# Windowed attention and a gated feed-forward on one core: first loads in one queue, four output parts and some deferred work at other places in a hand-written order

## The chip, the cores and the metric

One core of a Trainium2 chip. The metric is the device time of one execution in microseconds (us). Kernel before: median 245.3 us of 4 runs (244.92 to 245.75).

## The reference, cut to what matters

Attention over 4 batches, 8 heads, 768 positions and 64 numbers a head. A position sees the 96 positions up to itself and the first 8 ("global") ones. A linear bias by distance is added to the scores. The result, 3072 tokens of 512 numbers, goes through a feed-forward with 1536 inner numbers:

```python
scores = scale * np.matmul(q, k.transpose(0, 1, 3, 2)) + bias   # bias = -slope[h] * dist
a = softmax(np.where(keep, scores, -1e9))                       # keep: global or local
x = (a @ v).transpose(0, 2, 1, 3).reshape(B * S, H * D)
g = x @ w_gate
out = (g * sigmoid(g) * (x @ w_val)) @ w_out
```

## The kernel before, in words

**Tiles and blocks.** The 3072 tokens are 8 tiles of 384, two for each batch (the code's `b`). A tile's feed-forward has 12 blocks of 128 inner numbers, written (t, f) below. `gate_or_val` (L549) does one block in two calls: the first multiplies the tile by the gate weights (four matmuls of 128x384, tile `gps`), ScalarE takes a tanh of it (`th`, L558), and VectorE makes the SiLU (`sl`, L560); the second multiplies by the value weights (four matmuls, `vps`) and VectorE writes the product to `hT` (L564). `out_part` (L568) multiplies three blocks of a finished tile by `wo`; four parts make 128 tokens of output in the one bank `o0`, ScalarE copies that to `osb` (L582), and SP's queue stores it (L583). A tile has 12 parts.

**Attention beside it.** While one tile goes through the feed-forward, the attention of the next batch is put between its blocks as steps: `tr` transposes q and k of a pair of heads (TensorE, then copies on ScalarE and VectorE); `sc` multiplies keys by queries for two or three units (pair, key range); `va` makes, for four heads, the sums of the weights (`den`) and the two weighted sums of the values (`num`), and VectorE turns them into tokens: `dT` (L449), `dR` (L450), `rb` (L455) and two `xT` (L475). For batch 0, `sch` does bias and scores of a pair's second half, `trh` its transposes. From batch 1's second half on, `vas` does both groups of heads in one step.

**Order.** The order of every engine is the order in which the Python code issues. `stretches` lists the blocks with the number of output parts after each (`ff`, L766), and a dictionary of steps by place: (t, f) is behind block f and its parts, (t, f, n) ahead of the n-th part. Work that a step puts off lies in the list `later`: exponentials of the units behind the first, the multiplication by the masks (VectorE), and the four VectorE pieces of `va`. `run_later(1)` takes one piece: ahead of each gate, each value product and each output part. `take` empties the list ahead of a new step.

```python
            for which in range(2):
                run_later(1)
                gate_or_val(t, f, which, NC if t == 0 and f < 2 else 0)
```

**Banks.** `gps` and `vps` take turns in three PSUM banks x0 to x2 (`spare`); steps take turns in a0 to a3 (`banks`). A three-unit `sc` takes two of the spare banks for its first unit. From (0,9) to (1,2) `widen` (L803) lends the a banks to the feed-forward, so that seven take turns; `narrow` (L811) ends that, and gps(1,2) takes the bank that vps(1,0) used.

**Loads.** POOL's queue issues the converting loads in the order of the code, at most eight under way: weights by quarters of the blocks (`load_w`), `wo` in four loads of three blocks' rows each (`load_wo(g)`, g 0 to 3), q and k of batch 1 (`load_qk`), global rows (`load_globals`) and values (`load_v_rest`). The very first loads are unconverted: k32 on SP's queue, the identity and q32 on ScalarE's. SP's queue also stores the outputs and copies the global rows of v (`copy_globals`).

Of the kernel before, what the change touches and what calls it, by code (L numbers as in the profile page):

```python
# [37 lines left out]
def kernel(  # L38
# [12 lines left out]
    nc = tc.nc  # L51
# [48 lines left out]
    q32 = sb2.tile([128, 2, J2 * D], FP32, name="q32", tag="qst")  # L100
# [4 lines left out]
    def half_of(src, half, h0, h1):  # L105
        return src[0, h0:h1, TB * half:TB * half + TB, :].rearrange(
            "h (p j) d -> p h (j d)", p=128)
# [1 line left out]
    vG32 = sb.tile([NG, H, D], FP32, name="vG32")  # L109
    nc.sync.dma_start(out=k32, in_=half_of(k, 0, 0, 2))  # L110
    nc.scalar.dma_start(out=ident, in_=const_dr.ap()[:, 0:128])
    nc.scalar.dma_start(out=q32, in_=half_of(q, 0, 0, 2))
    nc.sync.dma_start(out=dist[:, 0:2 * WIN], in_=const_dr.ap()[:, 128:128 + 2 * WIN])
    nc.sync.dma_start(out=vG32, in_=v[0, :, 0:NG, :].rearrange("h p d -> p h d"))
    nc.sync.dma_start(out=dist[:, 2 * WIN:], in_=const_dr.ap()[:, 128 + 2 * WIN:])
# [31 lines left out]
    def stage(b):  # L147
        qst[b] = sb2.tile([128, H, J * D], FP16, name="qst", tag="qst")
        kst[b] = sb2.tile([128, H, J * D], FP16, name="kst", tag="kst")

    def load_qk(b, h0, h1):
        for st, src in ((kst[b], k), (qst[b], q)):
            nc.gpsimd.dma_start(
                out=st[:, h0:h1, :],
                in_=src[b, h0:h1].rearrange("h (p j) d -> p h (j d)", p=128))
# [23 lines left out]
    def load_globals():  # L179
        for dst, src in ((kG, k), (vG[:, 1:], v)):  # L180
            nc.gpsimd.dma_start(
                out=dst.rearrange("p b h d -> p (b h) d"),
                in_=src[1:, :, 0:NG, :].rearrange("b h p d -> p (b h) d"))
# [33 lines left out]
    def load_wo(g):  # L217
        nc.gpsimd.dma_start(
            out=wo[:, 3 * g:3 * g + 3, :],
            in_=moe_w_out[384 * g:384 * g + 384].rearrange("(f p) d -> p f d", p=128))  # L220
# [18 lines left out]
    def banks(name, dt=FP32):  # L239
        return [bank(name, dt) for _ in range(2)]  # L240

    def spare(name, dt=FP32):
        tag = state["x"][gv.get("n", 0) % len(state["x"])]
        gv["n"] = gv.get("n", 0) + 1
        return single(name, tag, dt)

    def single(name, tag, dt=FP32):
        return ps.tile([128, 512 if dt == FP32 else 1024], dt, name=name, tag=tag)
# [8 lines left out]
    def run_later(n):  # L257
        for _ in range(n):
            if later:
                later.pop(0)()  # L260
# [277 lines left out]
    def products(t, f, which, c0, c1, dst=None):  # L538
        if f == 0 and which == 0 and c0 == 0:
            hTs[t] = sb2.tile([128, NFF, TB], FP16, name="hT", tag="hT", bufs=3)  # L540
        if c0 == 0:
            if dst is None:
                dst = spare("gv"[which] + "ps")
            gv[f, which] = dst
        w = (wg, wv)[which]
        for c in range(c0, c1):
            nc.tensor.matmul(  # L547
                gv[f, which][:, 0:TB], lhsT=w[:, c, 128 * f:128 * f + 128],
                rhs=x_of(t)[:, c, :],  # L549
                start=(c == 0), stop=(c == NC - 1))  # L550

    def gate_or_val(t, f, which, c0=0):
        products(t, f, which, c0, NC)
        dst = gv.pop((f, which))

        if which == 0:
            th = sb2.tile([128, TB], FP32, name="th", tag="th")
            nc.scalar.activation(out=th, in_=dst[:, 0:TB], func=AF.Tanh, scale=0.5)  # L558
            sl = sb2.tile([128, TB], FP32, name="sl", tag="sl")
            nc.vector.scalar_tensor_tensor(  # L560
                out=sl, in0=th, scalar=1.0, in1=dst[:, 0:TB], op0=AluOp.add, op1=AluOp.mult)
            gv["sl"] = sl
        else:
            nc.vector.tensor_mul(hTs[t][:, f, :], dst[:, 0:TB], gv["sl"])  # L564
# [37 lines left out]
    for c in range(3):  # L602
        load_v_rest(0, c)
    nc.gpsimd.dma_start(
        out=vCut[NG:NG + cut], in_=v[0, :, 3 * KC:TB, :].rearrange("h p d -> p h d"))
# [41 lines left out]
    load_w(8, 12)  # L647
    load_wo(0)
    load_wo(1)
    stage(1)  # L650
    load_qk(1, 0, 4)
    load_globals()
    load_wo(2)
    load_wo(3)
    load_qk(1, 4, 8)
    for c in range(NCH):
# [29 lines left out]
    def sc(b, *units):  # L686
        def step():
            for i, (hp, bk, *other) in enumerate(units):
                pair = pairs[b + 1 if other else b, hp]
                on_vector = pair.b < 2 or bk < 2 or hp % 2 == 0  # L690
                exps, mask = pair.scores(
                    bk, nc.vector if on_vector else nc.gpsimd,
                    [spare("sc") for _ in range(2)] if len(units) == 3 and i == 0
                    else banks("sc"))
                if i == 0:
                    exps()
                else:
                    later.append(exps)
                later.append(mask)
        return step  # L700

    def va(b, g, half):
        return lambda: quads[b, g].values(half, bank, nc.vector)
# [4 lines left out]
    def tr(b, hp):  # L708
        return pairs[b, hp].transposes

    def trh(h0, h1, by_engine):
        def step():
            b0, b1 = single("trs", "o0", FP16), spare("trs", FP16)
            (a, b), (c, d) = [(t[:, 0:TB], t[:, TB:2 * TB]) for t in (b0, b1)]
            k_eng = V if by_engine else A
            pair_of = [(h0, (c, a)), (h1, (d, b))] if by_engine else [(h0, (b, a)), (h1, (d, c))]
            for hp, tr in pair_of:
                pairs[0, hp].turn_half(1, tr)
            for hp, tr in pair_of:
                pairs[0, hp].copy_half(1, tr, k_eng, A)  # L720
        return step

    def sch(hp):
        def step():
            p = pairs[0, hp]
            scs = [p.bias(1, 0), p.bias(1, 1)]
            for which in range(2):
                p.scores_half(1, which, scs[which], which == 1)
        return step
# [9 lines left out]
    def first(t, b):  # L739
        return {(t, 2): [tr(b, 0), tr(b, 1)],  # L740
                (t, 4): [sc(b, (0, 0), (0, 1), (1, 0))],
                (t, 6): [tr(b, 2), tr(b, 3)],
                (t, 7): [sc(b, (1, 1), (2, 0), (2, 1))],
                (t, 9): [sc(b, (3, 0), (3, 1))],
                (t, 10): [va(b, 0, 0)],
                (t, 11, 1): [va(b, 1, 0)]}

    def both(t, b):

        n = b + 1  # L750
        return {(t, 0): [sc(b, (0, 2), (1, 2), (2, 2)), fetch(n, 0, 1)],
                (t, 5): [sc(b, (3, 2), (0, 0, n), (1, 0, n)), fetch(n, 2, 3)],
                (t, 8): [vas(b, 1)],
                (t + 1, 0): [sc(n, (0, 1), (1, 1), (2, 0))],
                (t + 1, 4): [sc(n, (2, 1), (3, 0), (3, 1))],
                (t + 1, 8): [vas(n, 0)]}

    def second(t, b):
        return {(t, 0): [sc(b, (0, 2), (1, 2))], (t, 3): [sc(b, (2, 2), (3, 2))],
                (t, 7): [vas(b, 1)]}  # L760

    half1 = {(0, 1): [trh(0, 1, False)], (0, 2): [sch(0)],
             (0, 3): [sch(1), trh(2, 3, True)], (0, 5): [sch(2)], (0, 6): [sch(3)],
             (0, 7): [va(0, 0, 1)], (0, 8): [va(0, 1, 1)]}

    def ff(t, f0, f1, n_out=(0,)):  # L766
        return [(t, f, n_out[(f - f0) % len(n_out)]) for f in range(f0, f1)]

    stretches = [
        (ff(0, 0, 12), half1),  # L770
        (ff(1, 0, 5, (0, 0, 0, 0, 1)) + ff(1, 5, 11, (1,)) + [(1, 11, 5)], first(1, 1)),
        (ff(2, 0, 12, (1,)) + ff(3, 0, 12, (1,)), both(2, 1)),
        (ff(4, 0, 12, (1,)) + ff(5, 0, 12, (1,)), both(4, 2)),
        (ff(6, 0, 12, (1,)), second(6, 3)),
        (ff(7, 0, 12, (1,)), {})]

    loads, after = {}, {}

# [40 lines left out]
    def take(step_list):  # L819
        run_later(len(later))  # L820
        for step in step_list:
            step()

    for tiles, steps in stretches:
        for t, f, n_out in tiles:
            for ld in loads.pop((t, f), []):
                ld()
            if f == 0:
                while any(fn.__name__ in ("spread", "spread_first", "scale") for fn in later):
                    run_later(1)  # L830
            for which in range(2):
                run_later(1)
                gate_or_val(t, f, which, NC if t == 0 and f < 2 else 0)
                for fn in after.pop((t, f, which), []):
                    fn()
            for n in range(n_out):
                if (t, f, n) in steps:
                    take(steps.pop((t, f, n)))
                run_later(1)
                out_part(*outs.pop(0))  # L840
            if (t, f) in steps:
                take(steps.pop((t, f)))
        assert not steps
# [40 lines left out]
```

The softmax here doesn't subtract the row's maximum and nothing guards it: scores larger than these inputs give would overflow.

## Time and profile before

| | before |
|---|---|
| median of 4 runs | 245.3 us |
| the profiled execution: its own time / its span | 244.92 / 243.1 us |
| PE busy | 234.6 us, 96% of the span |
| VectorE (DVE) busy | 165.7 us, 68% |
| ScalarE (ACT) busy | 129.6 us, 53% |
| POOL busy | 96.6 us, 40% |
| granted TensorE clock | 9 tenths or more in all 40 slices |

The span runs from the first to the last instruction of the profiled execution. In a timeline row stand the start, the length, engine, line and operation, out<-in with shapes, the number of instructions merged into the row, and in brackets the idle time of the engine just ahead of it with what ended it. A row of the waits names who waited for whom, the total, how often, and the longest. A row's length in the timeline runs to the end of its last instruction; on PE, consecutive groups overlap in these lengths, and the distance between the starts of two rows tells what a group takes of the engine.

Where the stages lie: PE's first transposes start at 4.71 us, the first matmul of the feed-forward at 15.16, tile 1 begins at about 41.6, tile 2 at 74.4, and the last 24 matmuls begin at 237.3.

### The profile page before, as it was taken

The page shows a single profiled execution, that of the slowest core. Times are in us where ns is not written, and L with a number is a line of the kernel's source. Part 1 is how long each engine was busy: PE and PEld are TensorE (multiplying, and loading weights), DVE is VectorE, ACT ScalarE, POOL GpSimd, SP SyncE. Part 2 cuts the span into 40 slices and gives each one's busy share as a digit, 9 for nine tenths or more (in the row PEclk, how much of TensorE's full clock was granted, in tenths as well). Part 3 has the DMA queues.
Part 4 walks back from the last instruction along what each step waited for, and adds up shares of the span by engine and source line. Part 5 has one row for each costly group of instructions (what it writes and reads, how often), then busy time and mean ns, then how long its engine had stood idle before and what let it go on. Part 6 is the DMA issues. An engine that isn't in the chain of part 4 may idle for free.

```text
span 243.1 us, 6052 instructions
## 1 busy us (share of the span) xinstructions
PE 234.6 (96%) x2428; PEld 135.4 (56%) x2428; DVE 165.7 (68%) x354; ACT 129.6 (53%) x295; POOL 96.6 (40%) x117
## 2 busy tenths in 40 slices
PE   8899899799999999999999999999999999999994
PEld 4455466455555556555565556555655565555543
DVE  5665649879796768776786658776785568555610
ACT  5637586786864565366346464367336634333221
POOL 8899664737990000996062252700032213000000
PEclk9999999999999999999999999999999999999999
DMA  8999999999999574899319877941101101110122
GB/s 150 164 184 197 180 206 197 205 152 124 135 130 153 120 133 99 55 153 143 56 8 144 143 141 87 77 59 44 46 0 46 43 6 40 44 42 2 44 89 87
DMA packets 84612, 25.10 MB, mean 103 GB/s; under 512 B 72816, under 2 KB 81640, under 8 KB 84584
## 3 DMA queue, kind: packets, MB, share of 16 engines
q0 software_dynamic: 65296, 14.05, 67.0%
q1 hardware_dynamic: 18728, 10.30, 16.7%
q8 instruction: 19, 0.31, 0.5%
q10 hardware_dynamic: 560, 0.36, 0.5%
q14 instruction: 9, 0.07, 0.1%
HBM read 28.67 MB, written 6.29 MB: 144 GB/s over the span
## 4 chain that ended last, share of the span: by engine, by line
PE 84%; DMA 6%; POOL 5%; DVE 2%; issue 1%; ACT 0%; DVEq 0%; POOLq 0%
PE gps L547 25%; PE vps L547 24%; PE ops L576 23%; DMA wv<-in_moe_w_val_dram 4%; PE sc L379 3%; PE num L439 3%; DMA vS<-in_v_dram 3%; PE den L439 2%; POOL q L119 1%; PE trs L273 1%; POOL wg L213 1%; PE ops L592 1%; POOL k L119 1%; POOL wv L213 1%; DVE xT L475 1%
## 5 line engine op out<-in xcount | busy, mean ns | idle before, releaser
L547 PE MATMUL gps<-xT,wg 128*128 128x384 f16 x376 | 77.3, 327 | 2.6 <-DVE hT L564 1.7
L560 DVE SCALAR_TENSOR_TENSOR sl<-th,gps 128x384 f32<-128x384 f32 x94 | 51.9, 553 | 40.3 <-ACT th L558 39.8
L547 PE MATMUL vps<-xT,wv 128*128 128x384 f16 x376 | 76.6, 326 | 0.7 <-DMA wv<-in_moe_w_val_dram 0.6
L558 ACT ACTIVATE th<-gps 128x384 f32<-128x384 f32 x94 | 46.9, 499 | 53.2 <-PE gps L547 51.9
L576 PE MATMUL ops<-wo,hT 128*128 128x512 f16 x276 | 72.8, 379 | 0.0
L564 DVE TENSOR_TENSOR hT<-vps,sl 128x384 f16<-128x384 f32 x94 | 52.1, 554 | 8.8 <-PE ops L576 0.5
L547 PEld LDWEIGHTS <-wg 128*128 128x128 f16 x384 | 35.0, 98 | 33.8 <-issue 3.6
L547 PEld LDWEIGHTS <-wv 128*128 128x128 f16 x384 | 37.5, 98 | 26.8 <-issue 1.3
L576 PEld LDWEIGHTS <-hT 128*128 128x128 f16 x276 | 26.9, 98 | 23.9
L387 ACT ACTIVATE at<-sc 128x432 f16<-128x432 f32 x72 | 33.2, 539 | 11.5 <-PE sc L379 11.5
L516 POOL TENSOR_TENSOR xT<-ns,rb 128x384 f16<-128x384 f32 x10 | 9.8, 994 | 66.0 <-DVE rb L455 55.0
L171 POOL DMA_DIRECT2D vS<-in_v_dram x28 | 24.7, 899 | 5.0 <-DMA kst<-in_k_dram 3.0
L582 ACT ACTIVATE osb<-ops 128x512 f32<-128x512 f32 x23 | 13.7, 597 | 22.0 <-PE ops L576 22.0
L398 POOL TENSOR_TENSOR at<-at,masks 128x864 f16<-128x864 f16 x4 | 7.3, 1819 | 23.8 <-ACT at L387 19.1
L398 DVE TENSOR_TENSOR at<-at,masks 128x864 f16<-128x864 f16 x20 | 12.1, 605 | 5.7 <-ACT at L387 5.7
L194 POOL DMA_DIRECT2D kst<-in_k_dram x16 | 14.0, 896 | 2.9 <-PE gps L547 2.3
L361 ACT ACTIVATE at<-sc 128x432 f16<-128x432 f32 (+2 forms) x32 | 11.7, 447 | 5.0 <-PE sc L350 4.8
L194 POOL DMA_DIRECT2D qst<-in_q_dram x16 | 13.8, 891 | 0.2 <-issue 0.2
L512 ACT COPY ns<-num 128x384 f32<-128x384 f32 x20 | 8.1, 493 | 7.9 <-PE num L439 7.9
L439 PE MATMUL num<-at,vS 128*32 128x216 f16 (+6 forms) x560 | 11.1, 226 | 0.0
L395 DVE TENSOR_TENSOR at<-at,masks 128x432 f16<-128x432 f16 x24 | 8.1, 378 | 4.4 <-ACT at L387 4.4
L449 DVE STREAM_TRANSPOSE dT<-den 128x384 f32<-128x384 f32 x16 | 9.3, 581 | 1.6 <-PE den L439 1.1
(74 smaller groups left out, 178.5 us busy)
## 6 DMA issues: line engine op xcount, KB each, us to landing
out_dram<-osb SPq DMA_DIRECT2D x23, 256.0 KB
vS<-in_v_dram POOLq DMA_DIRECT2D x24, 120.0 KB, 5.3
wo<-in_moe_w_out_dram POOLq DMA_DIRECT2D x4, 384.0 KB, 10.5
qst<-in_q_dram POOLq DMA_DIRECT2D x16, 96.0 KB, 4.3
kst<-in_k_dram POOLq DMA_DIRECT2D x16, 90.0 KB, 4.2
wg<-in_moe_w_gate_dram POOLq DMA_DIRECT2D x4, 256.0 KB, 7.7
wv<-in_moe_w_val_dram POOLq DMA_DIRECT2D x4, 256.0 KB, 8.1
kst<-in_k_dram POOLq DMA_DIRECT2D x2, 384.0 KB, 11.7
```

Of the source, the lines that this page charges most:

```text
L171: nc.gpsimd.dma_start(out=vSs[b][NG:NG + n, c, :, :], in_=v[b, :, KC * c:KC * c + n, :].rearrange("h p d -> p h d"))
L194: nc.gpsimd.dma_start(out=st[b][p0:p0 + n, h // 2, :, h % 2, :], in_=src[b, h, 0:n * J].rearrange("(t p) d -> p t d", p=n))
L361: nc.scalar.activation(out=at[:, hi, 0:col + n], in_=sc[hi][:, 0:col + n], func=AF.Exp, scale=scale)
L387: nc.scalar.activation(out=at[:, hi, :], in_=sc[hi][:, 0:BANK], func=AF.Exp, scale=scale)
L398: mul_eng.tensor_mul(at, at, m[:, :, o:o + BANK])
L439: nc.tensor.matmul(dst[r, o:o + n], lhsT=ones[:, 0:32] if side is None else vals[:, 4 * g + j, side::2], rhs=pairs[b, 2 * g + j // 2].at[c ...
L547: nc.tensor.matmul(gv[f, which][:, 0:TB], lhsT=w[:, c, 128 * f:128 * f + 128], rhs=x_of(t)[:, c, :], start=(c == 0), stop=(c == NC - 1))
L558: nc.scalar.activation(out=th, in_=dst[:, 0:TB], func=AF.Tanh, scale=0.5)
L560: nc.vector.scalar_tensor_tensor(out=sl, in0=th, scalar=1.0, in1=dst[:, 0:TB], op0=AluOp.add, op1=AluOp.mult)
L564: nc.vector.tensor_mul(hTs[t][:, f, :], dst[:, 0:TB], gv["sl"])
L576: nc.tensor.matmul(ops, lhsT=hTs[t][:, f, 128 * i:128 * i + 128], rhs=wo[:, f, :], start=(f == 0), stop=(f == NFF - 1))
L582: nc.scalar.mul(out=osb, in_=ops, mul=0.5)
```

## The change

The edits, each on its own:

1. q32's load is issued on SP's queue, behind k32's, and no longer on ScalarE's.
2. The third load of `wo` is issued ahead of batch 1's first q and k loads and its global rows.
3. Output parts behind (0,10), (0,11), (1,0) and (1,2): four that were elsewhere. Before, tile 1 had one part behind (1,4) to (1,10) each and five behind (1,11). Now it has one behind (1,0), (1,2) and (1,4) to (1,9), two behind (1,10) and (1,11). Tile 7 has none behind (7,10) and (7,11).
4. In tiles 0 and 1 a put-off piece is run behind each gate and each value product, with the operations that follow them, and no longer ahead of them.
5. Batch 1's last three steps of its first half (scores of pair 3, and the values of both groups) stand one block earlier, and the two-unit `sc` of batch 1 takes spare banks for its first unit.

```diff
-    nc.scalar.dma_start(out=q32, in_=half_of(q, 0, 0, 2))
+    nc.sync.dma_start(out=q32, in_=half_of(q, 0, 0, 2))
...
     load_wo(1)
+    load_wo(2)
     stage(1)
     load_qk(1, 0, 4)
     load_globals()
-    load_wo(2)
     load_wo(3)
...
-                    [spare("sc") for _ in range(2)] if len(units) == 3 and i == 0
+                    [spare("sc") for _ in range(2)] if i == 0 and (len(units) == 3 or b == 1)
...
-                (t, 9): [sc(b, (3, 0), (3, 1))],
-                (t, 10): [va(b, 0, 0)],
-                (t, 11, 1): [va(b, 1, 0)]}
+                (t, 8): [sc(b, (3, 0), (3, 1))],
+                (t, 9): [va(b, 0, 0)],
+                (t, 10, 1): [va(b, 1, 0)]}
...
-        (ff(0, 0, 12), half1),
-        (ff(1, 0, 5, (0, 0, 0, 0, 1)) + ff(1, 5, 11, (1,)) + [(1, 11, 5)], first(1, 1)),
+        (ff(0, 0, 10) + ff(0, 10, 12, (1,)), half1),
+        (ff(1, 0, 4, (1, 0)) + ff(1, 4, 10, (1,)) + ff(1, 10, 12, (2,)), first(1, 1)),
...
-        (ff(7, 0, 12, (1,)), {})]
+        (ff(7, 0, 10, (1,)) + ff(7, 10, 12), {})]
...
             for which in range(2):
-                run_later(1)
+                if t > 1:
+                    run_later(1)
                 gate_or_val(t, f, which, NC if t == 0 and f < 2 else 0)
+                if t < 2:
+                    run_later(1)
```

## The prediction

> Notation: (t, f) is feed-forward block f of token tile t; gps and vps are its gate and value products, th, sl and hT the tanh, SiLU and product behind them. Starts are on the clock of the profiled execution of before.
>
> **What bounds it now.** I read the shares of the span first: PE is busy 234.6 of 243.1 us, at full granted clock in every slice. PE's matmuls are the same before and after, so only PE's waits can change the time. Next, the waits of PE:
>
> ```profile
> PE gps L547 <- DVE hT L564: 1.7, 1, 1.7
> PE warm L612 <- DVE kT L131: 1.2, 1, 1.2
> PE gps L547 <- DMA wg<-in_moe_w_gate_dram: 0.7, 2, 0.5
> PE vps L547 <- DMA wv<-in_moe_w_val_dram: 0.6, 1, 0.6
> ```
>
> The timeline of PE places them: weights at 20.0, 26.25 and 27.71; DVE's wait at (1,2):
>
> ```profile
> 43.59 0.81 PE L547 MATMUL vps<-xT,wv 128*128 128x384 f16 x4
> 46.14 0.81 PE L547 MATMUL gps<-xT,wg 128*128 128x384 f16 x4 [1.74 <-DVE hT L564]
> ```
>
> Four such matmuls begin 0.65 after the four before them, though a row shows 0.81: the next could have begun at 44.24, so the wait costs 1.90, not 1.74. (The Trainium skill, "Perfetto Trace Analysis", section "Tensor Engine Instruction", says that a matmul's end is estimated, not observed. By the row's end the wait is 1.74 and my sum 0.16 higher; the spacing of starts decides.)
>
> A second loss is not listed, because it lies inside a group, at (2,0):
>
> ```profile
> 74.38 1.10 PE L547 MATMUL gps<-xT,wg 128*128 128x384 f16 x4
> 75.32 0.81 PE L547 MATMUL vps<-xT,wv 128*128 128x384 f16 x4
> ```
>
> 0.94 from start to start in place of 0.65: 0.29 lost, to the last xT of VectorE (74.08, 1.03 long). Both losses are VectorE running late after it has turned sums into tokens. Its timeline ahead of the first:
>
> ```profile
> 35.84 0.57 DVE L449 STREAM_TRANSPOSE dT<-den 128x384 f32<-128x384 f32 x1
> 36.45 0.23 DVE L450 RECIPROCAL dR<-dT 128x12 f32<-128x12 f32 x1
> 36.68 0.55 DVE L560 SCALAR_TENSOR_TENSOR sl<-th,gps 128x384 f32<-128x384 f32 x1
> ...
> 40.56 1.03 DVE L475 TENSOR_TENSOR xT<-ns,rb 128x384 f16<-128x384 f32 x2
> 41.51 0.55 DVE L560 SCALAR_TENSOR_TENSOR sl<-th,gps 128x384 f32<-128x384 f32 x1
> ...
> 45.53 0.56 DVE L564 TENSOR_TENSOR hT<-vps,sl 128x384 f16<-128x384 f32 x1
> ```
>
> It has no gap from 34.71 to 47.2. 36.68 is sl(0,8), 41.51 sl(0,9), 45.53 hT(1,0), which frees the bank that gps(1,2) takes when the pool narrows back to three. Four blocks take 4.58: 1.12 each.
>
> **Part by part.** The instruction order of the changed kernel gives the moves.
>
> *First loads.* q32's issue (0.55 on ACT) goes behind k32's (0.46 on SP): issued at about 1.26 instead of 1.15; dist and vG32 0.5 later. Bytes are the same, and PE still meets the wv load that ends at 27.7: PE idles 0.47 and 0.65 just ahead of it, which absorbs a later head; an earlier head only waits longer. I take 0, with plus or minus 0.55, the moved issue, as ends. (The Trainium skill, "DMA: Bandwidth & Descriptors", section "Queues, rings and completion order", says that a DMA engine takes turns between queue rows. That speaks against one row: k32 and q32 would get one turn against POOL's, not two. ScalarE's conversion of q32 now starts 3.4 after its issue, VectorE's of k32 2.9; if q32 had to wait for half of k32's time the head would slip, as an estimate from this page and those rows, by some 1, and the sum by 0, as the 1.12 covers it.)
>
> *Put-off work behind tanh, tile 0.* Two effects.
> (a) ACT. sch(3)'s last biases need the banks that sch(2)'s two 432-column exponentials empty. Now four exponentials run in a row:
>
> ```profile
> 30.36 1.52 ACT L361 ACTIVATE at<-sc 128x264 f16<-128x264 f32 x4 [0.97 <-PE sc L350]
> 31.74 0.53 ACT L558 ACTIVATE th<-gps 128x384 f32<-128x384 f32 x1
> ```
>
> After, th(0,6) stands ahead of the last two. It can start when gps(0,6), 30.45 to 31.11, is done plus 0.2: 31.31. The exponentials start 0.39 later at 31.70 and 32.11, and end (0.54 each) at 32.24 and 32.65. The bias matmuls, now due at about 32.09 and 32.27, wait until 32.29 and 32.70: **+0.43** on PE.
> (b) DVE. dT and dR of (0,8), which fill 35.84 to 36.68 now, go behind sl(0,8). That waits for th(0,8), at 36.64 plus 0.43 = 37.07: DVE idles 1.2. From there sl .47, dT .61, dR .23, hT .47, rb .68, two xT .92, dT .61, dR .26, rb .68, two xT .95 (starts to starts in the rows above) = 5.88: sl(0,9) at 42.98, not 41.51. hT(1,0) ends 4.58 later: 47.56.
>
> *Four outputs.* One in each of (0,10), (0,11), (1,0), (1,2). The first three, 0.65 each, stand ahead of gps(1,2): PE arrives at 44.24 + 1.95 + 0.43 = 46.62 and finds the bank at 47.61 (0.05 of semaphore): wait 0.99 instead of 1.90: **-0.91**. The outputs are only moved: two are taken from (1,11), two from tile 7, so their own 2.60 net to nothing. Their cover: hT(0,11) ends at 46.4, needed at 48.9. wo(2), issued in kst's slot, should land near 41.6, when kst does now; needed at 44.7. wo(3) lands at 47.7 as now, needed at 48.9. If that cover of 1.2 is gone, PE waits one for one. The block-1 rows of q land about 2.2 later, at 45.6, for transposes at 49.7. On SP the three vS copies (44.11) now stand behind the first output's store, to about 50; va needs them near 66. In tile 7 two fewer outputs leave (7,11) bare: vps(7,11) needs sl(7,10), 1.97 after its gps, and arrives at 1.95: 0.
>
> *Tile 1's end.* From the transposes of (1,2) on I keep before's clock; everything is 2.13 later and two outputs ahead. hT(1,7), now behind no mask but a later sl, delays gps(1,8) by 0.08. At (1,8) the mask goes between sl and hT: sl 62.74, two masks 63.21 to 63.80, hT to 64.36. The scores of pair 3, one block sooner, take two of the three spare banks, so gps(1,9) needs the bank of hT(1,8): 64.41 against an arrival at 63.89: **+0.52** (with the 0.08, 0.60). The boundary: now
>
> ```profile
> 68.97 0.58 DVE L449 STREAM_TRANSPOSE dT<-den 128x384 f32<-128x384 f32 x1
> 69.58 0.23 DVE L450 RECIPROCAL dR<-dT 128x12 f32<-128x12 f32 x1
> 70.19 0.55 DVE L560 SCALAR_TENSOR_TENSOR sl<-th,gps 128x384 f32<-128x384 f32 x1 [0.38 <-ACT th L558]
> ```
>
> After: DVE runs dry at 67.92, waits for th(1,10) and starts sl(1,10) at 68.74. Then without a gap sl, dT, dR, hT, rb, two xT, dT, dR, sl(1,11), rb, hT(1,11): the last two xT end at 74.92 and 75.42. PE is at gps(2,0) at 73.58 (block 11 and two outputs since va), so vps(2,0) starts at 75.63 instead of 74.23: 1.40 lost, now 0.29: **+1.11**. The block sooner is paid back, because block 11's sl and hT (1.1) now lie in the chain and only two outputs, not four, cover it.
>
> *Later tiles.* Two outputs ahead, the output's copy (0.60 on ACT) falls between the second and third unit's exponentials after sc at (2,0), (3,0), (3,4), (4,0), (5,0), (5,4). Now:
>
> ```profile
> 78.64 1.79 ACT L387 ACTIVATE at<-sc 128x432 f16<-128x432 f32 x4
> 80.28 0.54 ACT L558 ACTIVATE th<-gps 128x384 f32<-128x384 f32 x1
> ```
>
> The copy starts at 79.55, 0.2 after its matmuls, and holds th to 80.87, sl(2,2) ends at 81.98, and vps(2,3) at 81.94 needs that bank: 0.05 to 0.09, six times: **+0.4** (ends 0 and 0.9).
>
> **Sum.** +0.43 - 0.91 + 0.60 + 1.11 + 0.4 = +1.6. The profiled execution took 244.92 (span 243.1 and 1.8 around it): 246.5. It is the fastest of four, whose median is 245.3; from that 246.9. I give 246.6.
>
> **Rivals**, from the median of 245.3.
> *Faster:* the reordering costs VectorE nothing. Place: its two dry spells ahead of sl(0,8) and sl(1,10), price 1.2 and 0.8. It decides once th(0,8) starts near 35.6 instead of 36.6 and th(1,10) as early against its work. Then sl(0,9) is at 41.9, the wait of 1.90 is gone, and the boundary loses 0.6: -1.90 + 0.3, nothing else: 243.7. Against: th follows gps by 0.2 in each row, and gps comes no sooner.
> *Cancelled:* the bank waits at sch(3) and (1,9) and the six small ones don't show (slack under 0.1 in my walk would do for the six, earlier exponentials for the others). (b) shrinks with (a). Left: -0.91 + 1.11 = +0.2: 245.5. For: each is a difference of two walked times. Against: no other bank is free there.
> *Worse, from the forecast's 246.6:* wo(3) or the first loads also slip past their cover, by 1 to 1.5: 247.9. Against: 1.1 to 1.2 of cover.
>
> **Numbers.** Chances: forecast 0.60 (half width 0.7), cancelled 0.20, faster 0.13, worse 0.07. A measurement can tell 0.3%, 0.74 us, from no change, so slower begins at 246.04. Forecast's low tail gives a little to "same": faster 0.13, same 0.23, slower 0.64. The range leaves out the faster case and the worse one's far part: 244.7 to 247.8.
>
> **What to look for after.** PE's wait on hT at (1,2) near 1.0, not 0; the bias matmuls of L339 at about 32 waiting for ACT; gps(1,9) waiting for hT; the group gps(2,0) 2 us long; VectorE idle ahead of sl(0,8) and sl(1,10); wv still landing near 27.7. I am wrong if VectorE has no such gaps, if gps(2,0) starts vps within 0.3 of its due time, or if a wait on wo appears.

## The result, and the profile after

The changed kernel takes 246.05 us (median of 43 runs, 245.50 to 246.78), the kernel before 244.75 us on the same chips (median of 64). The ratio is 1.0048, with a 95% interval of 1.0039 to 1.0057: 1.2 us slower (0.95 to 1.4). The 245.3 us that stood for the kernel before were the median of four runs, 0.55 above that of the 64.

The profiled execution of the changed kernel took 246.01 us, span 244.2, against 244.92 and 243.1: +1.1 in both. The granted clock was 1.000 in both. So its trace can be set beside the earlier one, time by time. Four rows of the waits of PE after (who waited for whom, total, times, longest):

```profile
PE trs L299 <- DMA q<-in_q_dram: 1.1, 1, 1.1
PE num L439 <- DVE dT L449: 0.6, 1, 0.6
PE gps L547 <- DVE hT L564: 0.4, 1, 0.4
PE gps L547 <- DVE xT L475: 0.4, 1, 0.4
```

The listed 1.7 for hT at (1,2) is gone. Three listed waits on VectorE stand in its place, and each is shorter than it. The list alone would promise a faster kernel; it leaves out what lies inside groups. (The q of the first row is the second load of q, on POOL's queue, and not q32.) The timeline of PE, after, in three places. First sch(3) and the values of batch 0:

```profile
31.88 1.28 PE L339 MATMUL sc<-dist,slopeI 128*128 128x72 f16 x6
33.09 0.48 PE L350 MATMUL sc<-qT,kT 64*128 64x72 f16 x10
...
37.34 0.49 PE L439 MATMUL den<-at,ones 128*32 128x72 f16 x20
38.42 0.79 PE L439 MATMUL num<-at,vS 128*32 128x72 f16 x40 [0.59 <-DVE dT L449]
```

The six bias matmuls of L339 take 1.21 from start to start; before, they took 0.69 (31.76 to 32.45): 0.52 lost, without a bracket. The second num matmuls wait for dT, which before they did not:

```profile
36.70 0.49 PE L439 MATMUL den<-at,ones 128*32 128x72 f16 x20
37.02 0.78 PE L439 MATMUL num<-at,vS 128*32 128x72 f16 x40
```

They start 1.08 after den, and before 0.32: 0.76 lost, where the bracket says 0.59.

Around (1,2):

```profile
46.95 0.81 PE L547 MATMUL vps<-xT,wv 128*128 128x384 f16 x4
47.63 0.81 PE L547 MATMUL gps<-xT,wg 128*128 128x384 f16 x4
...
48.93 0.81 PE L576 MATMUL ops<-wo,hT 128*128 128x512 f16 x3
49.67 0.53 PE L273 MATMUL trs<-ident,kst 128*64 128x128 f16 x12
```

gps(1,2), at 47.63, follows after 0.68: 0.03 of wait where there was 1.90. The transposes start at 49.67 against 47.53 before, +2.14, but with four outputs (2.60) ahead of them: PE is 0.46 ahead here. Then the end of tile 1:

```profile
65.44 0.54 PE L379 MATMUL sc<-qT,kT 64*128 64x216 f16 x8
66.43 0.81 PE L547 MATMUL gps<-xT,wg 128*128 128x384 f16 x4 [0.45 <-DVE hT L564]
...
75.78 0.49 PE L547 MATMUL gps<-xT,wg 128*128 128x384 f16 x2
76.65 0.79 PE L547 MATMUL gps<-xT,wg 128*128 128x384 f16 x2 [0.38 <-DVE xT L475]
77.28 0.81 PE L547 MATMUL vps<-xT,wv 128*128 128x384 f16 x4
```

gps(1,9) starts 0.99 after the scores, where the same pair of rows stood 0.48 apart before (65.36 and 65.84): 0.51 lost. The group gps(2,0) takes 1.50 in place of 0.65: 0.85 lost, before 0.29. vps(2,0) is at 77.28 against 75.32, +1.96 with two outputs more (1.30): now 0.66 behind. The last 24 matmuls start at 238.34 against 237.26, +1.08. So the account runs -0.46 at the transposes, +1.12 from there to tile 2, +0.42 in the later tiles: **+1.08**.

VectorE, after, at the two places where put-off work went behind a tanh:

```profile
37.32 0.55 DVE L560 SCALAR_TENSOR_TENSOR sl<-th,gps 128x384 f32<-128x384 f32 x1 [1.22 <-ACT th L558]
37.79 0.57 DVE L449 STREAM_TRANSPOSE dT<-den 128x384 f32<-128x384 f32 x1
...
43.00 0.55 DVE L560 SCALAR_TENSOR_TENSOR sl<-th,gps 128x384 f32<-128x384 f32 x1
...
70.77 0.56 DVE L560 SCALAR_TENSOR_TENSOR sl<-th,gps 128x384 f32<-128x384 f32 x1 [0.85 <-ACT th L558]
```

VectorE sits idle for 1.22 and 0.85 with dT ready to run (before, dT and dR filled all of the one and most of the other), and everything behind is that much later: sl(0,9) at 43.00, not 41.51, and hT(1,0) ends at 47.58.

### The profile page after: what moved, and what is told of

It is laid out like the page before. It is cut to its first block, busy times and chain, and to the rows that moved or that the text cites. A ratio compares the mean times of both kernels' runs of the same rounds, so it can differ in the third digit from the quotient of the medians.

```text
span 244.2 us, 6050 instructions
## 1 busy us (share of the span) xinstructions
PE 236.2 (97%) x2428; PEld 136.0 (56%) x2428; DVE 165.1 (68%) x354; ACT 129.9 (53%) x295; POOL 96.7 (40%) x117
## 3 DMA queue, kind: packets, MB, share of 16 engines
HBM read 28.67 MB, written 6.29 MB: 143 GB/s over the span
## 4 chain that ended last, share of the span: by engine, by line
PE 82%; DMA 6%; POOL 5%; DVE 3%; ACT 2%; issue 1%; POOLq 0%
PE gps L547 25%; PE vps L547 23%; PE ops L576 23%; DMA wv<-in_moe_w_val_dram 3%; PE num L439 3%; PE sc L379 3%; DMA vS<-in_v_dram 3%; PE den L439 2%; POOL q L119 1%; PE trs L273 1%; POOL wg L213 1%; PE ops L592 1%; POOL k L119 1%; POOL wv L213 1%; DVE sl L560 1%
## 5 line engine op out<-in xcount | busy, mean ns | idle before, releaser
L387 ACT ACTIVATE at<-sc 128x432 f16<-128x432 f32 x72 | 33.8, 534 | 9.2 <-PE sc L379 9.2
```

The lines of the kernel that those rows point to most:

```text
L387: nc.scalar.activation(out=at[:, hi, :], in_=sc[hi][:, 0:BANK], func=AF.Exp, scale=scale)
```

## The experiments

All were timed in five rounds beside the kernel before, which read 244.7 to 244.9 us in each set; ratios are to it.

**The put-off work ahead again in the changed kernel** (edit 4 undone); and edit 4 alone in the kernel before (the same lines the other way round):

```diff
-                if t > 1:
-                    run_later(1)
+                run_later(1)
                 gate_or_val(t, f, which, NC if t == 0 and f < 2 else 0)
-                if t < 2:
-                    run_later(1)
```

> The changed kernel with the put-off pieces run ahead of each gate and value product again; all else as changed. Theory (the order behind the tanh makes ScalarE and VectorE late and costs most of the loss): the bias matmuls of the last pair wait no more (0.5 less), gps(1,2) starts near 46.3 instead of 47.63 without a wait, the wait at gps(1,9) shrinks to about 0.25 and the one in gps(2,0) from 0.85 to about 0.7. Some 1.8 us faster than the changed kernel, 244.2 (ratio to the kernel before about 0.997). Rival (the order is neutral, the moved outputs and steps cost it): as the changed kernel, 246.0, ratio 1.005.

Measured: 244.43 us, ratio 1.0000 (0.9981 to 1.0020). Without edit 4 the change costs nothing; the rival's 1.005 is outside the interval, and so is the gain that the theory asked for (0.997). The waits went as the theory said or further: in its trace the bias matmuls take 0.69 again, num and gps(1,2) don't wait, and the loss is 0.24 at gps(1,9) (0.25 expected) and 0.34 in gps(2,0) (0.7 expected). But its head was late, with gps(0,5) at 28.97 against 28.17, and behind that vps(0,5) lost 0.89 to a wait for sl that the changed kernel doesn't have.

> The kernel before with only the put-off pieces moved behind each product in tiles 0 and 1. Theory: gps(1,2) starts near 47.6 instead of 46.14 (VectorE's sl(0,9) 1.4 later), and the last xT ahead of gps(2,0) comes 0.8 later because sl(1,11) now stands ahead of dT; sum +2.2, about 246.95 against 244.75 before, ratio 1.009. Rival (order neutral): ratio 1.000.

Measured: 246.67 us, 1.0077 (1.0049 to 1.0104). The edit by itself costs 1.9 us, and the theory's 1.009 is inside the interval. Its trace has, as the changed kernel's has, the long bias group, num's wait of 0.59 for dT and a wait of gps(2,0) for xT. At (1,2), with no outputs to fill it, the wait stays although VectorE is later: gps(1,2) at 48.31 after an idle time of 1.82, because PE arrives later too.

**Behind the tanh in tile 1 alone**, to part the two tiles' shares:

```diff
-                if t > 1:
+                if t != 1:
                     run_later(1)
                 gate_or_val(t, f, which, NC if t == 0 and f < 2 else 0)
-                if t < 2:
+                if t == 1:
                     run_later(1)
```

> The changed kernel with the pieces behind the tanh in tile 1 only, tile 0 as before. Theory (of the order's cost, tile 0 has 1.3, tile 1 some 0.5): gps(1,2) near 46.3, then all waits of the changed kernel (0.5 at gps(1,9), 0.85 in gps(2,0)): 1.3 faster than the changed kernel, 244.7, ratio 1.000. Rival (the cost lies in tile 1): 246.0, ratio 1.005.

Measured: 245.33 us, 1.0023 (1.0001 to 1.0044). Between the two: about 0.6 us for each tile, so neither the theory (1.3 in tile 0, ratio 1.000) nor the rival (all in tile 1, 1.005) is borne out; both ratios lie outside the interval, the theory's just. Its interval overlaps those of both neighbours, so the split is no firmer than that.

**q32 on ScalarE's queue again**, in the changed kernel; and edit 1 alone in the kernel before (the same lines the other way round):

```diff
-    nc.sync.dma_start(out=q32, in_=half_of(q, 0, 0, 2))
+    nc.scalar.dma_start(out=q32, in_=half_of(q, 0, 0, 2))
```

> The changed kernel with q32's load on ScalarE's queue again. Theory (the head's slip of 1.1 us, first gvps at 16.25 instead of 15.16, is absorbed by the wait for the wv load that ends near 27.7): the head comes 1.1 sooner, PE waits longer at 26 to 28, and the time stays within 0.2 of the changed kernel, 246.05. Rival (the slip counts): 245.0.

Measured: 245.72 us, 1.0039 (1.0022 to 1.0055): by the ratios 0.2 us below the changed kernel, within both intervals.

In the profiled executions of two of the kernels above the head was late (edit 4 undone, and behind the tanh in tile 1 alone; gps(0,5) at 28.97 and 29.33). The waits of PE of the latter have:

```profile
PE sc L339 <- DMA dist<-consts: 1.8, 1, 1.8
```

dist's load stands behind q32's on SP in the changed order. (In that execution the granted clock was also at 0.50 from 7.3 to about 14 us, so its head is not late by the wait alone.) From these two executions I formed the theory that edit 1 costs a good part of a microsecond wherever put-off work lies ahead, and tested it twice.

> The kernel before with q32's load behind k32's on SP's queue and nothing else. Theory (dist comes late in one queue, the head slips by more than the 1.4 us that PE waits for weights between 19 and 28): 1.0 to 1.8 slower, 246.2, ratio 1.006. Rival (the waits for weights absorb it): 244.8, ratio 1.000.

Measured: 245.35 us, 1.0011 (0.9992 to 1.0030). **That theory fell**: +0.3 us, and none is inside the interval.

> The changed kernel with two edits undone: q32's load on ScalarE's queue and the put-off pieces ahead of each product. Theory after the first four runs (with the pieces ahead of the tanh, the late head of the one-queue loads is no longer covered: the run with the pieces ahead had gps(0,6) 1.8 us later than the kernel before): the head comes back, the gain of the order stays: 1.5 below the run with the pieces ahead, 242.9, ratio to before 0.993. Rival (the order's cost is only as large as that run showed): 244.4, ratio 0.999.

(The diffs of edit 1 and edit 4 above, both in the changed kernel; the texts below call it e8_q_act_ahead.) Measured: 244.29 us, 0.9967 (0.9948 to 0.9986), between the theory's 0.993 and the rival's 0.999, with both outside the interval. It is faster than the kernel before and the changed one. From the kernel with edit 4 alone undone (1.0000) it differs by edit 1 alone: 0.8 us, with intervals that just overlap. So what edit 1 costs with the pieces ahead stays open: +0.3 in the kernel before, 0.8 here. The wait of vps(0,5) for sl is in the two profiled executions with a late head above and not in this one. Its timeline of PE says what stops it, and its VectorE shows that it isn't VectorE:

```profile
48.49 0.81 PE L576 MATMUL ops<-wo,hT 128*128 128x512 f16 x3 [1.12 <-DMA wo<-in_moe_w_out_dram]
```

```profile
41.21 0.55 DVE L560 SCALAR_TENSOR_TENSOR sl<-th,gps 128x384 f32<-128x384 f32 x1
...
45.95 0.56 DVE L560 SCALAR_TENSOR_TENSOR sl<-th,gps 128x384 f32<-128x384 f32 x1 [0.17 <-ACT th L558]
```

sl(0,9) is at 41.21 and VectorE is waiting again by 45.95; PE has no wait for it at (1,2). The fourth early output, due at 47.21, then meets wo(3), which lands at 48.45. This is the cover of 1.2 that the prediction had named for the wo loads. It is gone because PE comes 1.7 earlier than the prediction's 48.9 and the load 0.75 later than its 47.7.

**The fourth early output one block later**, in that kernel (e10_fourth_later below):

```diff
-        (ff(1, 0, 4, (1, 0)) + ff(1, 4, 10, (1,)) + ff(1, 10, 12, (2,)), first(1, 1)),
+        (ff(1, 0, 4, (1, 0, 0, 1)) + ff(1, 4, 10, (1,)) + ff(1, 10, 12, (2,)), first(1, 1)),
```

> The changed kernel with q32 back on ScalarE's queue and the put-off work back ahead of the tanh (as in e8_q_act_ahead, 0.9967 of the kernel before), and with the fourth early output behind block (1,3) instead of (1,2). In the trace of e8_q_act_ahead that fourth output waits 1.12 us for the landing of wo(3), at 48.49. Theory, the landing is now the bound there: a block later the output needs its weights 1.3 us later, so the wait goes whole: 244.29 - 1.1 = 243.2 us, ratio about 0.992. Rival, another wait takes its place (VectorE's hT ahead of gps(1,2) or its transposes, or a later landing): within 0.3 of e8, 244.2 us, ratio about 0.996.

Measured: 243.71 us, 0.9969 (0.9948 to 0.9990). The trace has no wait for wo any more and none in its place at (1,2) or (1,3), but the ratio is that of the kernel with the wait; only the median is lower, by 0.6. The theory's 0.992 is outside the interval and the rival's 0.996 inside, though no other wait took the place at (1,2) or (1,3). In the two traces the gain is there: from gps(0,5) to vps(2,0) this one takes 47.16 and the one with the wait 48.21, but its gps(0,5) came 0.55 later (28.30 against 27.75). One reading, argued only: wo(3) lands at much the same time in both (48.45 and 48.75), so with a later head the wait in the other kernel would have been shorter than in that one execution.

**Batch 1's last steps back** (edit 5 undone in the changed kernel):

```diff
-                    [spare("sc") for _ in range(2)] if i == 0 and (len(units) == 3 or b == 1)
+                    [spare("sc") for _ in range(2)] if len(units) == 3 and i == 0
...
-                (t, 8): [sc(b, (3, 0), (3, 1))],
-                (t, 9): [va(b, 0, 0)],
-                (t, 10, 1): [va(b, 1, 0)]}
+                (t, 9): [sc(b, (3, 0), (3, 1))],
+                (t, 10): [va(b, 0, 0)],
+                (t, 11, 1): [va(b, 1, 0)]}
```

> The changed kernel with batch 1's last steps at their old places, (1,9), (1,10) and (1,11,1), and the two-unit scores in the a banks; outputs and order as changed. Theory (with only two outputs behind block 11 the sums come too late, the sooner steps are what holds that): no wait at gps(1,9), but the last xT some 2.5 later, vps(2,0) near 79.2 instead of 77.28: 1.9 slower than the changed kernel, 248.0, ratio 1.0125. Rival (the sooner steps cost the 0.5 of gps(1,9) and bring nothing): 245.5, ratio 1.003.

Measured: 248.82 us, 1.0146 (1.0114 to 1.0178). That is 2.4 us above the changed kernel, but part of it is the clock: four of its six executions have a mean granted clock of 0.991 to 0.993 and take 248.8 to 249.4 us, and the two at full clock take 247.44 and 247.64, about 1.5 above the changed kernel. In the changed kernel all but five executions are at 0.998 or more. The profiled execution is one of the four: its granted clock is 0.50 from about 79 to 82.3 us. Up to vps(2,0), at 78.56, the clock was full, and the stretch from gps(0,5) to there is 1.57 longer than in the changed kernel (50.68 against 49.11), which fits the 1.5. That is what the earlier steps bring: without them only one output lies between the last sums and gps(2,0) (in (1, 11, 1) the parts count from 0, so the step is ahead of the second of two), and PE waits where the chain ends:

```profile
77.93 0.79 PE L547 MATMUL gps<-xT,wg 128*128 128x384 f16 x2 [1.71 <-DVE xT L475]
```

**The four early outputs back** (edit 3 undone; the six of (1,10) and (1,11) stay parted as two and four):

```diff
-        (ff(0, 0, 10) + ff(0, 10, 12, (1,)), half1),
-        (ff(1, 0, 4, (1, 0)) + ff(1, 4, 10, (1,)) + ff(1, 10, 12, (2,)), first(1, 1)),
+        (ff(0, 0, 12), half1),
+        (ff(1, 0, 4) + ff(1, 4, 10, (1,)) + [(1, 10, 2), (1, 11, 4)], first(1, 1)),
...
-        (ff(7, 0, 10, (1,)) + ff(7, 10, 12), {})]
+        (ff(7, 0, 12, (1,)), {})]
```

> The changed kernel without the four early outputs: one each behind (1,4) to (1,9), two behind (1,10), four behind (1,11), and tile 7 with one behind each block. Theory (the early outputs fill VectorE's lateness): gps(1,2) still near 47.6, now with a wait of about 2, the boundary at (2,0) covered, the copies of later tiles back between other pieces: +0.65 against the changed kernel, 246.7, ratio 1.008. Rival (the early outputs only move the wait): 245.9, ratio 1.005.

Measured: 247.46 us, 1.0105 (1.0077 to 1.0133): the outputs bring 1.4; the theory's 1.008 is inside the interval, the rival's 1.005 is not. Its PE at (1,2):

```profile
48.24 0.81 PE L547 MATMUL gps<-xT,wg 128*128 128x384 f16 x4 [1.82 <-DVE hT L564]
```

Its gps(0,5) was 0.60 later than the changed kernel's (28.77 against 28.17). Less that, gps(1,2) is at 47.64, and the changed kernel's is at 47.63. Three outputs more or less ahead of it don't move it: VectorE sets that time.

**wo(2) loaded where it was** (edit 2 undone in the changed kernel):

```diff
-    load_wo(2)
     stage(1)
     load_qk(1, 0, 4)
     load_globals()
+    load_wo(2)
```

> The changed kernel with wo(2) loaded where it was before, not in the earlier slot. Theory, the third early output's weights then land about 45.5 to 46 us and are needed near 45.65, and VectorE holds gps(1,2) to 47.6 anyway: 0 to +0.3 us, 246.05 to 246.35 us, ratio 1.005 to 1.006. Rival, the later issue also pushes wo(3) back and the fourth output waits for it past VectorE's time: +1 us, 247 us, ratio about 1.009.

Measured: 246.30 us, 1.0065 (1.0031 to 1.0100). PE waits for no wo load in its trace, so the rival's mechanism isn't there, though its time is inside the interval. In the changed kernel this edit is worth nothing that was seen.

**Four outputs behind (1,11)**, two more, in the changed kernel, and the same in the kernel with the fourth output later (e11_sixteen and e12_both):

```diff
-        (ff(1, 0, 4, (1, 0)) + ff(1, 4, 10, (1,)) + ff(1, 10, 12, (2,)), first(1, 1)),
+        (ff(1, 0, 4, (1, 0)) + ff(1, 4, 10, (1,)) + ff(1, 10, 12, (2, 4)), first(1, 1)),
...
-        (ff(7, 0, 10, (1,)) + ff(7, 10, 12), {})]
+        (ff(7, 0, 8, (1,)) + ff(7, 8, 12), {})]
```

> The changed kernel with two more outputs behind (1,11), four there in place of two, so that 16 parts are done by the end of tile 1 and the osb copies of the later tiles fall behind blocks 3, 7 and 11 again; tile 7 has fewer left. Theory, the wait of 0.85 us ahead of tile 2's first gate group is covered by the two outputs (1.30 us) and the later tiles' 0.4 us from the copies between two exponentials is gone, with about 0.1 back at blocks of tile 7 without an output: 246.05 - 1.1 = 245.0 us, ratio about 1.000. Rival, the wait and the copies cost nothing at the end (other waits take their place): 246 us, ratio about 1.005.

Measured: 249.98 us, 1.0222 (1.0188 to 1.0255). **A miss by 5 us, and both theories with it.** What was aimed at came: vps(2,0) starts at 77.71 with four outputs ahead, 0.43 later than with two (1.30), so the 0.85 is covered. But PE has a new wait, one of five alike, in tiles 2 to 6:

```profile
214.15 0.59 PE L576 MATMUL ops<-wo,hT 128*128 128x512 f16 x2
215.50 0.39 PE L576 MATMUL ops<-wo,hT 128*128 128x512 f16 x1 [0.75 <-DVE hT L564]
215.73 0.49 PE L547 MATMUL gps<-xT,wg 128*128 128x384 f16 x2
```

With 16 parts done by the end of tile 1, the part behind (t,11) is the fourth of tile t's own first 128 tokens. Its third matmul multiplies block 11, the block that PE has only just left and that VectorE has yet to write. From start to start the part takes 1.58 in place of 0.65: 0.93, five times, 4.65. With tile 7's bare block (gps at 232.61, the next at 234.30 in place of 233.91: 0.39), the covered 0.87 and the copies' 0.4 that is the +3.8 of its span (248.0 against 244.2). The changed kernel is two parts short of this: its part behind (t,11) ends at block 5.

> Both edits of e10_fourth_later and e11_sixteen: q32 on ScalarE's queue, put-off work ahead of the tanh, the fourth early output behind (1,3), four outputs behind (1,11). Theory: with the put-off work ahead the loss ahead of tile 2's first gate group is only 0.35 us (trace of e8_q_act_ahead) and the copies' share 0.4, with 0.1 back in tile 7: another -0.6 from e10, 242.6 us, ratio about 0.990. Rival, the outputs behind (1,11) are worth nothing once VectorE is less late there: as e10_fourth_later, 243.2 us, or a ratio of 0.992.

Measured: 247.21 us, 1.0104 (1.0076 to 1.0132), with the same five waits of 0.75. Less 4.65 it would be at 242.6, but a version with the cover and without these waits was not run.

## Why the prediction was right, point by point

The predicted 246.6 stands 0.55 above the measured 246.05, and the side was right. About 0.25 of that is the base: 246.6 less 1.6 is 245.0, and the 64 runs gave 244.75. The rest is the sum: the trace shows +1.08 of its +1.6, and the two medians differ by 1.30.

- **The wait at (1,2), and the four outputs.** VectorE's idle time ahead of sl(0,8) was 1.22 for 1.2, and the walk's end held to 0.02: sl(0,9) at 43.00 for 42.98, hT(1,0) to 47.58 for 47.56, gps(1,2) at 47.63 for 47.61. That it held so closely is luck, for two errors cancel: sl(0,8) started at 37.32 for 37.07, mostly because PE was 0.12 later at gps(0,5) and lost 0.09 more at sch(3), and from there to sl(0,9) it took 5.68, not 5.88. (The recorded 37.07 and 5.88 make 42.95, too.) Yet "PE's wait on hT at (1,2) near 1.0" was wrong: it was 0.03. The walk had missed a wait on PE's side: the second group's num needs a bank that the first group's dT has to empty (the row names dT), and dT now runs behind sl(0,8) (num at 38.42, 0.76 lost from start to start). With the 0.12 and the 0.09 that is PE's arrival at 47.60 in place of 46.62. The error cost the sum nothing, because VectorE sets gps(1,2), as the kernel with the outputs back shows; what PE lost earlier it did not wait later.
- **ACT's exponentials.** +0.43 predicted, 0.52 found at sch(3). The same loss at sch(2) (24.05, before 23.39) went into the waits for weights. On PE's way to (1,2), sch(3)'s loss too is only part of the arrival there; its +0.43 and the -0.91 make -0.48, and the trace has -0.46.
- **gps(1,8) and (1,9).** 0.08 and 0.52 predicted, 0.05 and 0.51 found. The bracket says 0.45: the distance between starts was again the better reading.
- **The boundary to tile 2: the term that was mis-sized.** 1.40 lost predicted, 0.85 found; the term +1.11 is +0.56. VectorE's idle time ahead of sl(1,10) was right (0.85 for 0.8), but its chain was walked too long. After:

```profile
71.86 0.23 DVE L450 RECIPROCAL dR<-dT 128x12 f32<-128x12 f32 x1
72.00 0.49 DVE L564 TENSOR_TENSOR hT<-vps,sl 128x384 f16<-128x384 f32 x1
72.41 0.56 DVE L455 STREAM_TRANSPOSE rb<-dR 128x384 f32<-128x384 f32 x1
73.01 1.03 DVE L475 TENSOR_TENSOR xT<-ns,rb 128x384 f16<-128x384 f32 x2
```

  From start to start dR holds VectorE for 0.14 when an independent operation follows, not for 0.23; hT and sl in that place take 0.41, not 0.47, and rb takes 0.60, not 0.68. From the start of sl(1,10) to the end of the last xT it took 6.29 (70.77 to 77.06), where the walk had 6.68 (68.74 to 75.42). The walk had taken its distances from rows of before, where these operations have other neighbours; with pieces laced between others they no longer apply. The walk in tile 0 has the same error (its 5.88), but there a late start hid it. The rest of the 0.55 is that the chain started 0.10 sooner and PE came 0.07 later than walked. This 0.55 is all but the rounding of the distance between +1.6 and +1.08.
- **Later tiles.** +0.4 predicted, +0.42 found. ScalarE at (2,0) to (2,2), after:

```profile
81.50 0.60 ACT L582 ACTIVATE osb<-ops 128x512 f32<-128x512 f32 x1
81.99 0.95 ACT L387 ACTIVATE at<-sc 128x432 f16<-128x432 f32 x2
82.81 0.51 ACT L558 ACTIVATE th<-gps 128x384 f32<-128x384 f32 x1
```

  The copy lies behind two of the exponentials and ahead of the last two, and th(2,2) comes at 82.81, as the prediction put it (80.87, and 1.96 later here), and vps(2,3) is 0.06 late (83.96 for a due 83.90). The other places fit in their sums: from one vps(t,0) to the next, tiles 2 and 4 (one place each) take 0.06 more than before, tiles 3 and 5 (two each) 0.13, tile 6 nothing: 0.38 in all.
- **The head.** 0 predicted. The first matmul of the feed-forward came 1.09 later (16.25 against 15.16); the waits for weights took nearly all of it back, and gps(0,5) was at 28.17 against 28.05. The estimate from the Trainium skill ("DMA: Bandwidth & Descriptors", "Queues, rings and completion order": a DMA engine takes turns between queue rows) was a slip of some 1, by a q32 that waits for half of k32's time, and a sum of 0. Its size came out, but by luck: ScalarE began to convert q32 sooner than before, at 4.09 against 4.56, and what PE waited 1.08 for was the second load of q, on POOL's queue, which landed at 7.83 against 6.15. The kernel with the fourth output one block later has q32 on ScalarE's queue and waits 0.89 for that same load. The timed runs put edit 1 at 0.2, 0.3 and 0.8 us in the three pairs that differ by it alone, so a sum of 0 is not shown either.
- **Covers.** wo(2) and wo(3) were in time here, wo(2) landing at 42.41 for an output at 45.65. But wo(3) landed at 48.66 and not at 47.7, for an output at 48.93: of the cover of 1.2 that was counted on, 0.27 was left. In the kernel with edits 1 and 4 undone it was used up.
- **Rivals.** "Cancelled" needed the bank waits not to show; they show. "Faster" needed th earlier; VectorE's two idle spells are there.

That edit 4 is the cause is shown by both directions: 1.2 us gained by undoing it (1.0048 to 1.0000), 1.9 lost by making it alone. Not settled: how its cost parts between tile 0 and tile 1, and what edit 1 costs beside it.

## What to carry to other kernels

Work that is put off is safest in front of the wait that it can fill: moved behind, it leaves its engine idle by that wait, and everything that reads its results, the banks too, is late by as much. Before outputs, copies or loads are used as filler, write down which block's result and which load's landing each of them reads, for every later tile that the shift reaches: two outputs more covered 0.85 once and cost 0.93 five times. And where one engine sets the end of a stretch, a lost half microsecond on the other costs nothing there, so a list of waits before and after can't be summed: compare starts at marks that both kernels pass.

## What the runs showed of the hardware

The landing of the first loads, each a few hundred nanoseconds to issue, varies by as much as the whole change. The eight kernels with q32 on SP's queue issue their first loads alike, and in one profiled execution of each the first bias matmul waited for dist between 0.05 and 1.77 us; the one with 0.05, the changed kernel, then waited 1.08 for the second load of q. In none of the six with q32 on ScalarE's queue did PE wait for dist. The first matmul of the feed-forward came between 15.85 and 18.33 us in the eight and between 15.02 and 16.01 in the six; at gps(0,5), behind the waits for weights, the two lie at 27.71 to 29.33 and 27.63 to 28.84. So these waits take much of it back, though not always all. A single profile of the head misled me here; it took timed runs to see how little of it reaches the end in the kernel before.

The granted clock fell to 0.50 inside two of the 14 profiled executions, each time within about 1 us of PE's start after a stop: from about 79 to 82.3 us behind the 1.71 at gps(2,0), which ended at 77.93 (batch 1's last steps back), and from 7.3 to about 14 us behind the 1.77 for dist, which ended at 6.83 (behind the tanh in tile 1 alone). Stops of like length in others (1.74 in the kernel before, 1.82 with the outputs back) passed at 1.00. So a wait can cost more than its length; that the stop is the cause, and what decides it, was not tested.
